# Loads of v moved to GpSimd's queue, output sums in single-bank tiles, and a retuned list schedule, in an attention plus two-MLP kernel

## The chip, the cores and the metric

One core of one Trainium2 chip runs the whole program. The metric is the device time of one execution in microseconds (us), the median of several runs; lower is better.

## What is computed

Attention with a threshold, and then two MLPs, on 4 batches, 8 heads, 576 rows and head size 64 (2304 tokens of width 512, inner width 2048):

```python
scores = scale * np.matmul(q, k.transpose(0, 1, 3, 2))
thresh = np.max(scores, axis=-1, keepdims=True) - tau
scores = np.where(scores >= thresh, scores, -1000000000.0)
scores = scores - np.max(scores, axis=-1, keepdims=True)
attn = np.exp(scores)
attn = attn / (np.sum(attn, axis=-1, keepdims=True) + 1e-09)
x = np.matmul(attn, v)            # heads side by side: (2304, 512)
h = x @ w_in;  g = np.maximum(h, 0.0) + alpha * np.minimum(h, 0.0);  x = g @ w_out
h = x @ w2_in; g = h - np.tanh(h);                                   out = g @ w2_out
```

## The kernel before, in words

The kernel does not run its loops in the order in which they are written. Each piece of work is recorded with `add` (in `Plan`, from line 78): the engines that may do it with a planned duration for each, a rank, what it reads and writes, which PSUM banks it touches, and which tile buffers it takes. `Plan.order` then makes a list schedule: at each step it looks on every engine at the pieces whose inputs are planned to be there, takes the piece that can start first, and among equally early ones the one of lowest rank; where a piece may run on several engines, the engine on which it is planned to start first gets it, after a penalty (`POOL_PEN`, `ACT_PEN`, `DVE_PEN`). The constants at the top of the file (`TA`, `PA`, `PB`, `MLP_PE`, `MLP_G`, `PREP`, `XR`, `OFF`) make the ranks. The instructions of each engine stand in the program in exactly the order found, and each engine works through its own in that order.

The work itself, by stages:

- Attention goes by units: a pair of heads and a block of 256 queries (`prep`, `attend`, `attended`; the 64 left-over queries of a pair in `attend_left`). TensorE makes scores in the PSUM tiles `sc0` and `sc1` (L703, left-over ones L692); VectorE takes row maxima (L576) and a threshold (L579); ScalarE applies it (L305) and the exponential (L586), after which the score tile is free again; VectorE and ScalarE write the weights as two halves of 16 bits (L300, L617, L621), SyncE's queue transposes them by DMA (L631), and TensorE multiplies them by v (L682). The first four units go a shorter way (L597 to L600, L733 to L745).
- v comes by one DMA per head (`load_v`, L550, tile `vs`, three buffers); all but the first four units split it in two more pieces (`rest`, L555, on VectorE or GpSimd). q and k come by L507 and L515, and are split in a high and a low part (L302 or L300 high, L308 low).
- The first MLP's weights come as 32 blocks of 128x512 doubles (`piece`). Each is rebuilt and split by a chain of five steps: L305 and L374 or L372 ("three"), L377 ("middle"), a high part (L300 or L302, tile `i` or `o` and its last block `i3b` and the like) and a low part (L308). The rank of a block is PA plus PB times its number.
- While attention goes on, blocks of 256 tokens that are done pass through the first MLP: input products (`h_pair`, L918, into `hp` or `pt`), and output products (`acc_pair`, L1143, into `acc`). The last two blocks go together (`wide_products`, L1107).
- The second MLP multiplies by a scheme of seven products (`out_products`, L1035, and L1042 for two pairs that go plainly). Its output sums stand in four PSUM banks. Those are the two halves each of `sc0` and `sc1`, which by then serve attention no more: `half_bank` and `two_banks` cut them out. At a block's end ScalarE copies one sum (L300) and VectorE adds up the rest (L1068), and SyncE's queue stores the rows (L1088, L1092 for the last block).
- At the start TensorE gets 220 matmuls that compute nothing of use (`warm`, L1192) wherever the schedule has nothing better.

Of the kernel before, what the change touches and what calls it, by code (L numbers as in the profile page):

```python
# [9 lines left out]
F32 = mybir.dt.float32  # L10
# [21 lines left out]
KW, VW = S, 5 * D  # L32
# [9 lines left out]

TA = 69.2859
PA, PB = -14.922, 21.7041
MLP_PE = 1954.1131
MLP_G = -1037.3118
PREP = 2416.5189
WHOLE, SOLO, NATIVE = 4, 0, 4  # L50
FLEX_R = 1
TX = 240
# [13 lines left out]
FLEX = 1
T_WARM = 0.3
N_WARM = 110
DVE_PEN = 0.5807
OFF = {"KS": -791.84, "S": -573.01, "M": -4327.05, "TH": -2173.26, "E": -1574.86, "X": -552.67, "R": -2860.41, "N": -5093.87, "NL": -258.85, "F": -1836.12, "DT": -6146.31, "T": 21.16, "H": 2659.35, "AV": -799.7, "XC": -548.69, "XH": -2968.53}  # L70
DMA_LAG = 2.2
DMA_RATE = 230e3
BUFS = {
# [165 lines left out]
def attention_mlp_mlp(ctx: ExitStack, tc: tile.TileContext, kv, q0, q1, tau, w1i, w1o, alpha, w2i, w2o, out):  # L239
# [11 lines left out]
    add = plan.add  # L251
# [21 lines left out]

    sc = [ppool.tile([P, 1024], F32, name=f"sc{k}") for k in range(2)]
    acc = [ppool.tile([P, 512], F32, name=f"acc{t}") for t in range(2)]
    hp = ppool.tile([P, 2, BLK], F32, name="hp")
    pt = ppool.tile([P, 4, P], F32, name="pt")

    hps = hp, pt.rearrange("p (k c) s -> p k (c s)", k=2)

# [6 lines left out]
    ROOM = ("room", 0)  # L289
    T = {}  # L290
# [29 lines left out]
    space = []  # L320
# [174 lines left out]
    def prep(u, rank):  # L495
# [48 lines left out]
        for a in range(2) if k == u else ():  # L544
            n = (k, a)
            vs, v3 = ("vs", n), ("v3", n)

            def load_v(e, a=a, vs=vs):
                x = take(tpool, vs, [P, 2, 5, D], F32, "vs", BUFS["vs"])
                e.dma_start(out=x[:, 0], in_=kv[b, h + a][:, S:].rearrange("p (c d) -> p c d", c=5))  # L550

            def rest(e, part, vs=vs, v3=v3):
                x = T[vs][:, part]
                out_ = take(tpool, v3, [P, 5, D], BF16, "v3", BUFS["v3"]) if part else T[vs][:, 1]
                e.tensor_tensor(out=out_, in0=x, in1=x.bitcast(BF16)[:, :, 1::2], op=ALU.subtract)  # L555

            add({"SYNC": rate * VW}, rank - 6, load_v, [ROOM], [(*vs, 0)], takes=[("vs", vs)], lag=DMA_LAG)
            if not one(u):
                for part in range(2):
                    add(either(0.4, 0.7), rank, lambda e, part=part, f=rest: f(e, part), [(*vs, part), ROOM], [v3 if part else (*vs, 1)],  # L560
                        takes=[("v3", v3)] if part else [])
# [449 lines left out]

    def half_bank(n):
        k = {1: 0, 6: 1, 2: 2, 3: 3, 7: 4, 5: 5, 4: 6, 8: 7}[n]
        return sc[k // 4][:, k % 4 * BLK:(k % 4 + 1) * BLK], k // 2

    def two_banks(k):
        return sc[k // 2][:, k % 2 * 512:(k % 2 + 1) * 512]

    def out_products(p, rank):
        m, n = p // NPAIR, p % NPAIR  # L1020
# [58 lines left out]
        for t in (1, 0):  # L1079
            x = 3 - 2 * t  # L1080

            def both(e, t=t, x=x):
                total(e, T[o[t]], two_banks(x), T[o[t]])

            def store(e, t=t):
                if m < 2 * NBLK - 1:
                    row = (m - NBLK) // 2 * S + (m - NBLK) % 2 * BLK + t * P
                    e.dma_start(out=out[row:row + P, :], in_=T[o[t]])  # L1088
                else:
                    for k in range(2):  # L1090
                        row = (2 * t + k + 1) * S - D
                        e.dma_start(out=out[row:row + D, :], in_=T[o[t]][k * D:(k + 1) * D, :])  # L1092

            z = oa + ob if t else oc + od
            add({"DVE": 0.6}, r, both, [("c", x), *z], z, [("c", x)])
            add({"SYNC": 1.2}, r, store, z, [("out", m, t)], lag=3.0)

    def wide_products(p, rank):
        f = p - (NBLK - 2) * NPAIR
        banks = [acc[0], acc[1], two_banks(2), two_banks(3)]  # L1100
        keys = [("acc", 0), ("acc", 1), ("c", 2), ("c", 3)]
        for c in range(4):
            def emit(e, c=c):
                gh, gl = (T["g", p][:, part] for part in range(2))
                hi, lo = (weight(0, "o", part, f // 4)[:, f % 4, c * P:(c + 1) * P] for part in range(2))
                for n, (w, g) in enumerate(((hi, gh), (hi, gl), (lo, gh))):
                    e.matmul(banks[c], lhsT=w, rhs=g, start=(f == 0 and n == 0), stop=(f == NF - 1 and n == 2))  # L1107

            reads = [("w", (0, "o", f // 4), f % 4, part) for part in range(2)]
            add({"PE": 0.69}, rank + MLP_PE, emit, [*reads, ("g", p, 0), ("g", p, 1)], [keys[c]], [keys[c]])  # L1110
        if f < NF - 1:
            return
        for c in (2, 3, 0, 1):
            o = ("o", 2 * (NBLK - 2) + c)
# [208 lines left out]
```

## Time and profile before

| | us |
|---|---|
| median of 3 runs (lowest to highest) | 1052.99 (1048.88 to 1056.25) |
| the profiled execution | 1052.28 |
| its span, first to last instruction | 1050.5 |
| TensorE busy / idle in the span | 1024.3 / 26.2 |
| VectorE busy | 773.1 |
| ScalarE busy | 617.6 |
| GpSimd busy | 75.0 |
| mean granted TensorE clock | 0.993 of full |

In the profile, PE is TensorE's matmuls, PEld its weight loads, DVE is VectorE, ACT is ScalarE, POOL is GpSimd and SP is SyncE; a q behind an engine's name is its queue of DMA issues. A tile's name stands before an arrow, what it is made of behind it. "Idle" is the time an engine stood still before an instruction, and the name behind the arrow is what ended that wait. TensorE is at 2.4 GHz where the granted clock is 1.00 and at 1.2 GHz where it is half.

### The profile page before, as it was taken

Reading aid. Unit: us, or ns where it says so; the run is one execution under the profiler, and the core shown is the slowest. Engines: PE = TensorE matmul, PEld = TensorE weight load, DVE = VectorE, ACT = ScalarE, POOL = GpSimd, SP = SyncE. Lnnn points to the kernel's source line nnn. Section 1 sums busy time; section 2 is a strip of 40 time slices with the busy share of each in tenths; the row PEclk is TensorE's granted clock in tenths of the full one; section 3 lists DMA queues with packets and bytes.
Section 4 is the critical chain, followed back from the end, with each engine's and each line's share of the span. In section 5 each row is a group of like instructions: output and inputs, shape, how many; then the busy total and the mean of one; then the engine's idle time right before and its main releaser. Section 6 shows DMA issues by size and latency. Waiting matters only on the chain.

```text
span 1050.5 us, 22471 instructions
## 1 busy us (share of the span) xinstructions
PE 1024.3 (98%) x8859; PEld 928.7 (88%) x8859; DVE 773.1 (74%) x1738; ACT 617.6 (59%) x1287; POOL 75.0 (7%) x101
## 2 busy tenths in 40 slices
PE   9979889999999999999999999999999999999997
PEld 7759879999989999998999888998898898899886
DVE  6999989878878778887867787674584484485465
ACT  6988988788878788887746554442312222331321
POOL 0122121011110111101100000000000000000000
PEclk9989989999999999999999999999999999999999
DMA  6678988667876657775575343200010010010000
GB/s 201 185 180 192 214 204 172 131 117 153 149 135 135 131 120 146 146 124 119 98 218 185 130 126 115 81 21 1 21 41 21 21 41 21 21 41 21 1 21 21
DMA packets 188889, 110.75 MB, mean 105 GB/s; under 512 B 158688, under 2 KB 171248, under 8 KB 188784
## 3 DMA queue, kind: packets, MB, share of 16 engines
q1 hardware_dynamic: 188480, 108.51, 44.6%
q8 instruction: 69, 1.13, 0.5%
q10 hardware_dynamic: 304, 0.82, 0.3%
q14 instruction: 36, 0.29, 0.1%
HBM read 61.58 MB, written 9.96 MB: 68 GB/s over the span
## 4 chain that ended last, share of the span: by engine, by line
PE 59%; DVE 2%; ACT 2%; issue 1%; DMA 0%; SPq 0%; DVEq 0%; ACTq 0%
PE sc L1035 13%; PE hp L918 10%; PE acc L872 6%; PE pt L918 5%; PE acc L1143 5%; PE sc L1042 5%; PE pt L872 3%; PE hp L872 3%; PE pt L682 2%; PE sc L1107 2%; PE acc L1107 2%; PE sc L703 1%; DVE st L576 1%; ACT e L305 1%; ACT e L586 0%
## 5 line engine op out<-in xcount | busy, mean ns | idle before, releaser
L918 PE MATMUL hp<-x,i 128*128 128x256 f32 (+1 forms) x1584 | 231.5, 291 | 10.8 <-ACT e L305 5.3
L918 PEld LDWEIGHTS hp<-x,i 128*128 128x128 f32 x1584 | 206.5, 191 | 22.4 <-ACT e L305 5.6
L1143 PE MATMUL acc<-g,o 128*128 128x256 f32 x1232 | 165.7, 279 | 0.4 <-POOL g L308 0.4
L1143 PEld LDWEIGHTS acc<-g,o 128*128 128x128 f32 x1232 | 152.7, 188 | 3.9 <-POOL g L308 0.6
L305 ACT ACTIVATE e<-sc,st,qscale 128x576 f32<-128x576 f32 x144 | 118.0, 828 | 33.0 <-DVE st L579 20.8
L1035 PE MATMUL sc<-wp,g 128*128 128x256 f32 x756 | 135.9, 280 | 0.0
L1035 PEld LDWEIGHTS sc<-wp,g 128*128 128x128 f32 x756 | 115.8, 188 | 1.3
L576 DVE TENSOR_REDUCE st<-sc 128x1 f32<-128x576 f32 x144 | 102.7, 750 | 13.4 <-PE sc L703 12.5
L586 ACT ACTIVATE e<-e,natau 128x576 f32<-128x576 f32 x144 | 110.9, 774 | 0.2
L621 DVE SCALAR_TENSOR_TENSOR rw<-e,st,rw 128x576 f16<-128x576 f32 x128 | 103.6, 827 | 9.2 <-ACT rw L300 8.4
L1035 PE MATMUL sc<-wp,rw 128*128 128x256 f32 x378 | 106.1, 281 | 0.8 <-ACT o L300 0.8
L300 ACT ACTIVATE rw<-e,st 128x576 f16<-128x576 f32 x103 | 77.9, 771 | 16.7 <-DVE st L592 7.4
L300 ACT ACTIVATE g<-mr 128x512 fp32r<-128x512 f32 (+1 forms) x99 | 59.1, 597 | 47.8 <-PE sc L1107 16.6
L682 PE MATMUL pt<-eT,vs 128*64 128x256 f16 (+1 forms) x1584 | 72.6, 246 | 0.9 <-DMA eT<-rw 0.9
L1035 PEld LDWEIGHTS sc<-wp,rw 128*128 128x128 f32 x378 | 71.2, 188 | 2.3 <-ACT o L300 1.0
L308 DVE TENSOR_TENSOR g<-mr,g 128x512 fp32r<-128x512 f32 x80 | 55.6, 695 | 19.3 <-ACT g L300 18.4
L682 PEld LDWEIGHTS <-vs 128*64 128x64 bf16 x1584 | 64.5, 111 | 5.3 <-issue 1.0
L703 PE MATMUL sc<-kh,qh 64*128 64x320 f32 (+1 forms) x672 | 62.9, 314 | 4.3 <-ACT e L305 4.1
L872 PE MATMUL acc<-x,i 128*128 128x512 f32 x264 | 65.5, 395 | 0.0
L703 PEld LDWEIGHTS sc<-kh,qh 64*128 64x128 f32 x672 | 50.0, 188 | 13.5 <-ACT e L305 5.1
L872 PEld LDWEIGHTS acc<-x,i 128*128 128x128 f32 x264 | 48.9, 187 | 11.4
L918 PE MATMUL pt<-x,i 128*128 128x256 f32 (+1 forms) x352 | 58.0, 311 | 0.0
(247 smaller groups left out, 1708.4 us busy)
## 6 DMA issues: line engine op xcount, KB each, us to landing
vs<-in_kv_dram SPq DMA_DIRECT2D x58, 160.0 KB, 2.9
rw<-in_w1o_dram SPq DMA_DIRECT2D x16, 512.0 KB, 4.6
rw<-in_w2i_dram SPq DMA_DIRECT2D x16, 512.0 KB, 4.7
rw<-in_w2o_dram SPq DMA_DIRECT2D x16, 512.0 KB, 3.9
rw<-in_kv_dram SPq DMA_DIRECT2D x56, 144.0 KB, 2.9
rw<-in_w1i_dram SPq DMA_DIRECT2D x15, 512.0 KB, 4.9
out_dram<-o SPq DMA_DIRECT2D x16, 256.0 KB, 2.0
x1d<-o SPq DMA_DIRECT2D x14, 256.0 KB, 2.7
```

What stands on the lines that cost most here:

```text
L300: e.activation(out=out_, in_=in_, func=AF.Copy, **({} if scale is None else {"scale": scale}))
L305: e.activation(out=out_, in_=in_, func=AF.Prelu, alpha=alpha, **kw)
L308: e.tensor_tensor(out=out_, in0=in_, in1=hi.bitcast(F32), op=ALU.subtract)
L576: e.tensor_reduce(out=T[st][:, 0, j:j + 1], in_=x(s), axis=AX.X, op=ALU.max, negate=True)
L586: e.activation(out=w_, in_=w_, func=AF.Exp, bias=natau, scale=1.0, accum_out=T[st][:, 2, j:j + 1])
L621: e.scalar_tensor_tensor(out=x_[:, S + D:], in0=w_, scalar=r, in1=x_[:, :S], op0=ALU.mult, op1=ALU.subtract)
L682: e.matmul(po[HALVES[a]], lhsT=plane((k, a), part, c), rhs=eT(a, block), start=(i == 0), stop=(i == len(TERMS) - 1), skip_group_check=True)
L703: e.matmul(to(a, c), lhsT=x[HALVES[a], s], rhs=y[HALVES[a], c], start=(i == 0), stop=(i == len(terms) - 1))
L872: e.matmul(hq[k], lhsT=weight(1, "i", part, f // 4)[:, c, (f % 4) * P:(f % 4 + 1) * P], rhs=slots_of_x[x][:, :, c, :], start=(n0 + i == 0) ...
L918: e.matmul(hq if both_blocks else hq[:, k, :], lhsT=weight(l, "i", part, f // 4)[:, c, (f % 4) * P:(f % 4 + 1) * P], rhs=slots_of_x[x][:, ...
L1035: e.matmul(out_, lhsT=x[:, a], rhs=y[:, b], start=(begins and i == 0 and number in (1, 2, 5, 4)), stop=(n == NPAIR - 1 and i == 2), skip_g ...
L1143: e.matmul(acc[t][:, (c % 2) * BLK:(c % 2 + 1) * BLK], lhsT=w[:, c * P:(c + 1) * P], rhs=g[:, k, :], start=(f == 0 and n == 0 and c % 2 == ...
```

## The change

Four edits in one. The loads of v are recorded for GpSimd, with a planned 1.2 us each, in place of SyncE's queue. The output sums of the second MLP get four tiles of one bank each (`out0` to `out3`), for which the pool that holds `sc0` and `sc1` is released when the first of them is asked for. `SLACK` goes from 0 to 0.067: among pieces that can start up to 67 ns after the earliest, the lowest rank wins. And the ranks and penalties are new numbers.

```diff
-TA = 69.2859
-PA, PB = -14.922, 21.7041
+TA = 67.5699
+PA, PB = -1048.431, 17.9757
...
-POOL_PEN = 0.7718
-ACT_PEN = 0.0
+POOL_PEN = 0.4091
+ACT_PEN = 0.0556
...
-SLACK = 0
+SLACK = 0.067
...
-DVE_PEN = 0.5807
+DVE_PEN = 0.2845
...
-    sc = [ppool.tile([P, 1024], F32, name=f"sc{k}") for k in range(2)]
...
+    spool = tc.alloc_tile_pool(name="spool", bufs=1, space=PSUM)
+    sc = [spool.tile([P, 1024], F32, name=f"sc{k}") for k in range(2)]
+    banks_of_out = []
...
-            add({"SYNC": rate * VW}, rank - 6, load_v, [ROOM], [(*vs, 0)], takes=[("vs", vs)], lag=DMA_LAG)
+            add({"POOL": 1.2}, rank - 6, load_v, [ROOM], [(*vs, 0)], takes=[("vs", vs)], lag=DMA_LAG)
...
-        return sc[k // 4][:, k % 4 * BLK:(k % 4 + 1) * BLK], k // 2
+        return two_banks(k // 2)[:, k % 2 * BLK:(k % 2 + 1) * BLK], k // 2
...
-        return sc[k // 2][:, k % 2 * 512:(k % 2 + 1) * 512]
+        if not banks_of_out:
+            spool.release()
+            mpool = ctx.enter_context(tc.tile_pool(name="mpool", bufs=1, space=PSUM))
+            banks_of_out.extend(mpool.tile([P, 512], F32, name=f"out{n}") for n in range(4))
+        return banks_of_out[k]
```

What the new numbers do shows in the order of the instructions. On VectorE, around the last block of the first MLP's fourth input quarter (its low part is written to `i3b`), before:

```order
L555 TENSOR_TENSOR v_2_1977<-vs_1792 128x320
L308 TENSOR_TENSOR i_1811<-tw_1914,i_1811 128x512
L374 TENSOR_SCALAR rw_1857<-rw_1857 128x512
L589 TENSOR_SCALAR st_1842<-st_1842 128x2
L576 TENSOR_REDUCE st_1993<-sc_90 128x1
L592 RECIPROCAL st_1842<-st_1842 128x2
L377 SCALAR_TENSOR_TENSOR tw_1987<-tw_1987,rw_1857 128x512
L579 TENSOR_SCALAR st_1993<-st_1993,qscale,atau 128x1
L302 TENSOR_SCALAR i_1811<-tw_1987 128x512
L756 SCALAR_TENSOR_TENSOR x_96<-pt,x_95 128x256
L308 TENSOR_TENSOR i3b<-tw_1987,i_1811 128x512
```

and now, on VectorE (lines are two higher here):

```order
L379 SCALAR_TENSOR_TENSOR tw_1839<-tw_1839,rw_1770 128x512
L623 SCALAR_TENSOR_TENSOR rw_1822<-e_1722,st_1559,rw_1822 128x576
L310 TENSOR_TENSOR last<-rw_1090,last 64x64
L557 TENSOR_TENSOR vs_1836<-vs_1836 128x320
L310 TENSOR_TENSOR i3b<-tw_1839,i_1653 128x512
```

with two of its steps now on ScalarE:

```order
L307 ACTIVATE tw_1839<-rw_1770 128x512
L374 ACTIVATE rw_1770<-rw_1770 128x512
L307 ACTIVATE e_1845<-sc_96,st_1830,qscale 128x576
L588 ACTIVATE e_1845,st_1830<-e_1845,natau 128x576
L302 ACTIVATE i_1653<-tw_1839 128x512
```

The step "three" (L374 before, on `rw_1857`) and the high part (L302) of this block went from VectorE to ScalarE, and the block's last instruction, the 270th on VectorE before, is the 240th now.

On GpSimd, in the stretch where the units with three-part v begin, before:

```order
L374 TENSOR_SCALAR rw_797<-rw_797 128x512
L302 TENSOR_SCALAR qh_916<-rw_829 128x256
L308 TENSOR_TENSOR o_879<-tw_884,o_879 128x512
L308 TENSOR_TENSOR last<-rw_716,last 64x64 x2
L555 TENSOR_TENSOR vs_899<-vs_899 128x320
L555 TENSOR_TENSOR v_1_1007<-vs_899 128x320
```

and now:

```order
L552 DMA vs_806<-in_kv_dram 128x320
L304 TENSOR_SCALAR qh_840<-rw_763 128x256
L310 TENSOR_TENSOR qh_840<-rw_763,qh_840 128x256
L557 TENSOR_TENSOR vs_806<-vs_806 128x320
L310 TENSOR_TENSOR o_801<-tw_855,o_801 128x512
L304 TENSOR_SCALAR o_801<-tw_922 128x512
L304 TENSOR_SCALAR kh<-rw_763 128x576
L552 DMA vs_1018<-in_kv_dram 128x320
L310 TENSOR_TENSOR qh_899<-rw_827,qh_899 128x256
L552 DMA vs_1029<-in_kv_dram 128x320
L310 TENSOR_TENSOR g_1040<-mr,g_1040 128x512
L557 TENSOR_TENSOR vs_1018<-vs_1018 128x320
```

The loads of v (L552) stand between splits of q, k, weights and g. Over the whole program GpSimd goes from 93 to 201 instructions beside its preamble: 58 loads and 50 more splits.

On TensorE, the last matmuls of the program, the plain pair of the last block's output, before:

```order
L1042 MATMUL sc0_89<-wp0_10255,g_1_13500 128x512 x2
L1042 MATMUL sc0_89<-wp1_10256,g_1_13500 128x512
L1042 MATMUL sc0_89<-wp0_10255,g_1_13500 128x512 x2
L1042 MATMUL sc0_89<-wp1_10256,g_1_13500 128x512
L1042 MATMUL sc1_90<-wp0_10255,g_1_13500 128x512 x2
L1042 MATMUL sc1_90<-wp1_10256,g_1_13500 128x512
L1042 MATMUL sc1_90<-wp0_10255,g_1_13500 128x512 x2
L1042 MATMUL sc1_90<-wp1_10256,g_1_13500 128x512
```

and now:

```order
L1048 MATMUL out1_105<-wp0_10278,g_1_13511 128x512 x2
L1048 MATMUL out1_105<-wp1_10279,g_1_13511 128x512
L1048 MATMUL out1_105<-wp0_10278,g_1_13511 128x512 x2
L1048 MATMUL out1_105<-wp1_10279,g_1_13511 128x512
L1048 MATMUL out3_107<-wp0_10278,g_1_13511 128x512 x2
L1048 MATMUL out3_107<-wp1_10279,g_1_13511 128x512
L1048 MATMUL out3_107<-wp0_10278,g_1_13511 128x512 x2
L1048 MATMUL out3_107<-wp1_10279,g_1_13511 128x512
```

The twelve matmuls are the same, but they write tiles of their own (`out1`, `out3`), while ScalarE's copy and VectorE's first four sums read `out0` and `out2`.

## Rows read from the trace of the kernel before

**Rows 1.** Part 1 of the page: busy time of three engines, share, instructions.
```profile
PE 1024.3 (98%) x8859; PEld 928.7 (88%) x8859; DVE 773.1 (74%) x1738; ACT 617.6 (59%) x1287; POOL 75.0 (7%) x101
```

**Rows 2.** Six stretches: us; PE, PEld, DVE, ACT, POOL busy; PEclk, DMA share, GB/s.
```profile
0.00:60.00 60.00, 58.95 (x497) 44.02 (x499) 48.46 (x117) 48.07 (x98) 8.11 (x18) 1.00 0.68 205
60.00:140.00 80.00, 67.58 (x718) 61.73 (x714) 74.89 (x163) 70.32 (x148) 17.52 (x21) 0.92 0.84 189
140.00:200.00 60.00, 58.42 (x636) 54.34 (x634) 52.58 (x111) 52.15 (x109) 9.51 (x10) 0.99 0.78 169
200.00:500.00 300.00, 295.65 (x3366) 280.20 (x3363) 245.55 (x537) 245.59 (x536) 36.51 (x50) 1.00 0.71 134
500.00:1000.00 500.00, 499.17 (x3361) 448.51 (x3360) 321.85 (x739) 191.16 (x377) 3.36 (x4) 1.00 0.21 64
1000.00:1050.50 50.50, 44.57 (x295) 39.84 (x293) 29.74 (x74) 10.31 (x22) 0.00 (x0) 0.98 0.08 22
```

**Rows 3.** Who PE waited for, the longest: us in total, times, longest.
```profile
PE hp L918 <- ACT e L305: 5.3, 2, 4.4
PE sc L703 <- ACT e L305: 4.1, 5, 1.2
PE hp L918 <- DVE i L302: 2.1, 1, 2.1
```

**Rows 4.** Timeline of PE around its two stalls: start us, us, what, [idle before].
```profile
74.78 2.68 PE L918 MATMUL hp<-x,i 128*128 128x256 f32 x11 [4.35 <-ACT e L305]
...
123.35 1.06 PE L703 MATMUL sc<-kh,qh 64*128 64x320 f32 x11 [1.16 <-ACT e L305]
...
125.65 2.16 PE L682 MATMUL pt<-eT,vs 128*64 128x256 f16 x36
...
130.78 1.06 PE L692 MATMUL sc<-kh,last 128*128 128x320 f32 x6 [1.28 <-ACT e L305]
...
134.49 0.80 PE L918 MATMUL hp<-x,i 128*128 128x256 f32 x2 [2.07 <-DVE i L302]
```

**Rows 5.** One stretch, DVE alone: us, DVE busy (instructions), PEclk, DMA share, GB/s.
```profile
0.00:134.70 134.70, 118.98 (x270) 0.97 0.76 194
```

**Rows 6.** View of tile vs: count, ns min/median/max, first to last start.
```profile
L550 SPq DMA_DIRECT2D vs<-in_kv_dram x58: 327/424/1249, 4.7 to 530.2; - x58
...
L555 DVE TENSOR_TENSOR vs<-vs x32: 475/490/962, 57.2 to 533.5; 128x320 f32<-128x320 f32 x32
L555 POOL TENSOR_TENSOR vs<-vs x18: 713/722/2175, 70.5 to 517.2; 128x320 f32<-128x320 f32 x18
```

**Rows 7.** The loads of v, L550: us from issue to landing.
```profile
DMA to landing us min/median/max: 2.1/2.9/7.8
```

**Rows 8.** Timeline: a second load of a unit on SP, and that unit's first product.
```profile
264.93 1.73 SPq L550 DMA_DIRECT2D vs<-in_kv_dram  x2
...
275.19 2.16 PE L682 MATMUL pt<-eT,vs 128*64 128x256 f16 x36
```

**Rows 9.** What POOL waited for, the longest entry.
```profile
POOL qh L308 <- ACT qh L300: 85.9, 10, 15.1
```

**Rows 10.** Timeline of the program's end on PE.
```profile
1041.44 0.96 PE L1042 MATMUL sc<-wp,g 128*128 128x512 f32 x3 [0.47 <-ACT o L300]
1042.98 0.97 PE L1042 MATMUL sc<-wp,g 128*128 128x512 f32 x3 [0.57 <-DVE o L1068]
1044.22 1.67 PE L1042 MATMUL sc<-wp,g 128*128 128x512 f32 x6 [0.28 <-DVE o L1068]
```

**Rows 11.** The same end on DVE.
```profile
1042.50 2.47 DVE L1068 TENSOR_TENSOR o<-sc,o 128x256 f32<-128x256 f32 x5 [2.81 <-PE sc L1042]
1045.93 0.69 DVE L1068 TENSOR_TENSOR o<-sc,o 128x512 f32<-128x512 f32 x1 [0.97 <-PE sc L1042]
```

More of the change, by code (lines that the diff above doesn't have):

```diff
@@ L41 @@
 STRASSEN = (0, 2, 3, 4, 5, 6)
-TA = 69.2859
-PA, PB = -14.922, 21.7041
-MLP_PE = 1954.1131
-MLP_G = -1037.3118
-PREP = 2416.5189
+TA = 67.5699
+PA, PB = -1048.431, 17.9757
+MLP_PE = 1433.9332
+MLP_G = -1384.7596
+PREP = 2365.4859
 WHOLE, SOLO, NATIVE = 4, 0, 4
@@ L64 @@
 GRP = 2
-XR = -5767.685
+XR = -5410.2762
 FLEX = 1
@@ L68 @@
 N_WARM = 110
-DVE_PEN = 0.5807
-OFF = {"KS": -791.84, "S": -573.01, "M": -4327.05, "TH": -2173.26, "E": -1574.86, "X": -552.67, "R": -2860.41, "N": -5093.87, "NL": -258.85, "F": -1836.12, "DT": -6146.31, "T": 21.16, "H": 2659.35, "AV": -799.7, "XC": -548.69, "XH": -2968.53}
+DVE_PEN = 0.2845
+OFF = {"KS": -535.86, "S": 778.7, "M": -3424.39, "TH": -4738.67, "E": -2104.47, "X": 647.63, "R": -3288.83, "N": -2846.97, "NL": 1041.57, "F": -2998.86, "DT": -6288.94, "T": 881.05, "H": 1417.61, "AV": 252.54, "XC": -843.71, "XH": -2688.93}
 DMA_LAG = 2.2
@@ L1091, in store @@
                         row = (2 * t + k + 1) * S - D
-                        e.dma_start(out=out[row:row + D, :], in_=T[o[t]][k * D:(k + 1) * D, :])
+                        e.dma_start(out=out[row:row + D, :], in_=T[o[t]][HALVES[k], :])
             z = oa + ob if t else oc + od
@@ L1099, in wide_products, with home_of @@
         f = p - (NBLK - 2) * NPAIR
-        banks = [acc[0], acc[1], two_banks(2), two_banks(3)]
+        def home_of(c):
+            return acc[c] if c < 2 else two_banks(c)
         keys = [("acc", 0), ("acc", 1), ("c", 2), ("c", 3)]
@@ L1106, in emit @@
                 for n, (w, g) in enumerate(((hi, gh), (hi, gl), (lo, gh))):
-                    e.matmul(banks[c], lhsT=w, rhs=g, start=(f == 0 and n == 0), stop=(f == NF - 1 and n == 2))
+                    e.matmul(home_of(c), lhsT=w, rhs=g, start=(f == 0 and n == 0), stop=(f == NF - 1 and n == 2))
             reads = [("w", (0, "o", f // 4), f % 4, part) for part in range(2)]
@@ L1116, in drain @@
             def drain(e, c=c, o=o):
-                copy(e, take(apool, o, [P, 512], F32, "o", BUFS["o"]), banks[c])
+                copy(e, take(apool, o, [P, 512], F32, "o", BUFS["o"]), home_of(c))
             def store(e, c=c, o=o):
```

## The prediction

> **What bounds the kernel now.** I read the share of busy time first, then a table by stretches, then the list of TensorE's waits, and last the timeline at the two places where TensorE stands still. TensorE is busy 98% of the span and no other engine over 74% [rows 1], so only TensorE's lost time can be won, 26.2 us of idle, and what a low clock costs. The table by stretches says where that is [rows 2]. From 500 to 1000 us TensorE lacks 0.83 us: no gain there, whatever the order. From 200 to 500 it lacks 4.35 us. From 60 to 140 it lacks 12.42 us, at a mean granted clock of 0.92, which is full speed with two stretches at half (1.2 instead of 2.4 GHz), each behind a long wait. In that same stretch VectorE is busy 74.9 of 80 us and ScalarE 70.3: they bound it, by what they must finish before TensorE can go on. From 0 to 60 TensorE looks full, but part of that is the 220 warm-up matmuls; VectorE and ScalarE set the pace there too (48 of 60 us each, of which the first 10 are loads). The end lacks 5.93 us.
>
> The waits agree: TensorE waits longest for ScalarE to free a score tile and for a weight block's high part from VectorE [rows 3]. The timeline has them at 74.78 (4.35 us), and from 123 to 134.49 (1.16, 1.28, 2.07 us) [rows 4]. The last of these is the fourth input quarter of the first MLP: its high part is on VectorE behind softmax work.
>
> **The change part by part.** The sum is made against the profiled execution, 1052.28 us (span 1050.5 and 1.78 outside); it lies 0.7 below the median of 1052.99, which I let go.
>
> *The new ranks, 60 to 140 us.* The block's last VectorE instruction ends some 0.7 us after 134.70, and is the 270th on VectorE; by 134.70 VectorE had been busy 118.98 us, so it had been idle 15.7 us since the start [rows 5]. In the new order it is the 240th. Priced kind by kind with the durations of before (an instruction that changed engine at the mean of its kind on the new one), the VectorE work up to it is 107.9 us in place of 119.6: 11.7 us less. But TensorE comes to that matmul with less work behind it too. Four attention steps that stood ahead of it now stand behind it: one scores, one products, one left-over scores and one left-over products, 6.0 us together (the first three begin in rows 4 with 1.06, 2.16 and 1.06 us, a few matmuls each not counted). So the block is ready 11.7 us earlier and wanted 6.0 us earlier: 5.7 us less waiting at most. Against it stands GpSimd: 53 of its instructions now stand ahead of that point where 28 did, and they disturb VectorE. The same split that takes VectorE 490 ns at the median took 962 ns at the worst [rows 6], so each of the 25 costs VectorE between nothing and 0.47 us, 0 to 11.8 us. I let 7 of the 25 collide, 3.3 us, since the median shows no delay at all. That leaves 2.4 us, and with no collision 5.7; I take 3.5, as the half-clock stretch that follows the wait goes with it in part. Both ends are kept: -5.7 to +6.1 (all 25 collide).
>
> *The first 70 us.* At the 11th scores matmul, for which both orders have put the same work on TensorE, VectorE has 2.5 us and ScalarE 4.4 us more ahead than before, counted in the same way, since high parts of weights went to ScalarE. That scores matmul will be 2.5 to 4.4 us later. I cost it at nothing: right behind it the old order waits 4.35 us for ScalarE [rows 4], and in the new one the matmul that waits there has 0.9 us of VectorE work and 3.5 us of ScalarE work more ahead, less than the 4.35, so the delay falls into that wait. If the wait does not shrink, 4.4 us are lost.
>
> *200 to 500 us.* With 8 to 13 us less work ahead on VectorE and ScalarE at equal TensorE progress (counted between 240 and 300 us of TensorE work), the waits there should shrink. TensorE lacks 4.35 us [rows 2]; what remains are waits for freed tiles, so I take 1.2 of it, between 0 and 4.35.
>
> *The loads of v.* 58 issues leave SyncE's queue, 0.42 us each [rows 6]; TensorE waits for none of that queue's transposes for long, so nothing is gained. On GpSimd no row shows a DMA issue. Below, it is no dearer than the shortest on SyncE, 0.33; above, than the longest GpSimd instruction over the same 320 columns, 2.18 [rows 6]; nearest is the median of that instruction, 0.72. Total GpSimd work becomes 75 [rows 1] + 50 splits (32 us) + 58 x 0.72 (42 us) = 149 us within 540 us: no bound. What counts is lateness. A unit's second load must wait for a buffer that the unit before frees, and is wanted soon: issued at 264.93, first used at 275.19, 10.3 us [rows 8]. Over the 25 second loads from the fifth unit on, that time has a median of 9.7 us and 4.3 us at the shortest. The chain in it is 2.9 us to landing [rows 7] and two splits of 0.49 [rows 6], 3.9 us, so 5.8 us are spare. While such a load waits for its buffer, splits of q, k, weights and g stand behind it on GpSimd, and TensorE's scores and input products wait for those. I cost it at nothing, covered by those 5.8 us; gone, that cover costs a us per us and unit.
>
> GpSimd and VectorE do lock each other out: the 713 ns split took 2175 ns once [rows 6], 1.46 us more. If every load were late by that, two of the 25 would be too late or just in time, about 1.1 us in all. The Trainium skill, page "SBUF — State Buffer", section "SBUF: two separate sides", speaks against this edit: a DMA from GpSimd's queue needs descriptors that GpSimd writes itself, and it cannot write them while VectorE holds the shared port; the section below it, "A bandwidth-pool intuition that's wrong", gives 3100 ns for a load that takes 620 alone. By that figure each load would be 2.5 us late, three of the 25 would run out of their spare time, for an estimated 3.5 us, and the sum would be 1049.4. The trace agrees that the two engines lock; no run here yet shows a DMA from that queue.
>
> *Single-bank tiles.* In the middle of the second MLP they win nothing (0.83 us in 500). At the end they do. The last twelve matmuls stand still three times, 0.47, 0.57 and 0.28 us, for ScalarE and VectorE reading the other bank of the same tile, and start up anew each time [rows 10]; they end at 1045.89, 4.9 us after the work before them. In one run, at the pace of the last six (1.67 us for 6), they take some 3.2 us: 1.7 less. VectorE's last sum waits for them (0.97 us) [rows 11]; its five sums before it then run beside the matmuls, done by about 1043.9, so the matmuls still end last. -1.7 us, between -1.3 (the idle alone) and -2.0.
>
> *Sum:* 1052.28 - 3.5 - 0 - 1.2 - 1.7 = 1045.9, or 1046.
>
> **The rivals.**
>
> *All stalls go (faster).* For it: the deficit of the fourth quarter, 5.7 us, is larger than the wait of 2.07 us it shows. Then the 12.42 us of 60 to 140 go but for the first wait of 4.35 (8.1), and so do 1.6 of the next 60 us and 1.3 after [rows 2], and 1.7 at the end: 12.7 less, 1039.6. Against it: the first 70 us are heavier than before.
>
> *Only the end is won (no change).* VectorE is lengthened by the doubled GpSimd work, or ScalarE's 4.4 us at the start are never caught up; then the 3.5 and the 1.2 fall away and 1050.6 stays. For it: VectorE is at 94% from 60 to 140, so each lengthening shows in full. The lock-out of loads by VectorE, 1.1 us by the rows, ends here too.
>
> *Late v (slower).* GpSimd works in order, and has stood 15.1 us in a single wait for ScalarE [rows 9]. A load of v behind such a wait comes late, and TensorE stands before that unit's products. It decides from 5.8 us of delay on, where the spare time is used up. At 6.4 us on the mean over 25 units it costs 25 x 0.6 = 15 us; with the end's gain and no other, 1052.28 + 15 - 1.7 = 1065.6. Against it: the ten waits of that row are 8.6 us on the mean, and in the new order few loads stand behind a split that waits for ScalarE.
>
> **How the numbers follow.** The forecast (1042.5 to 1049) has 0.46, all stalls gone 0.24, only the end 0.18, late v 0.12. One per cent, about what a measurement of this kernel can tell from no change, is 10.5 us: below 1042.5 is faster, above 1063.5 slower. All of the second case and a rest of the first, 0.07, fall below: 0.31 faster. Late v is split, 0.10 above: 0.10 slower, 0.59 within. The range goes from 1037 (the second case with some 2 us more of 200 to 500) to 1059 (the no-change case with the load delays and most of the 6.1 us of collisions); the forecast's own is 1042.5 to 1049.
>
> **What would show it.** Right: in the table by stretches 60 to 140 lacks some 9 us in place of 12.4, one of the two half-clock stretches is shorter or gone, and the wait for the fourth quarter's high part is no longer listed; the last twelve matmuls run without a gap. Wrong: a wait of TensorE's products for `vs` or its splits, or waits of scores for `kh` from GpSimd, among the longest; VectorE's split at over 0.49 us at the median; a DMA issue on GpSimd that takes over 2 us; a first wait at 75 us as long as before and the scores matmul behind 73.

## The result, and the profile after

| | before | after |
|---|---|---|
| median, us (lowest to highest, runs) | 1052.04 (1048.88 to 1056.25, 4) | 1065.18 (1064.12 to 1065.82, 4) |
| ratio, 95% interval | | 1.0120 (1.0104 to 1.0137) |
| the profiled execution / its span | 1052.28 / 1050.5 | 1065.82 / 1064.0 |
| TensorE busy / idle in the span | 1024.3 / 26.2 | 1031.9 / 32.1 |

The changed kernel is 1.2% slower, 13.1 us. The forecast was no change, 1046.0, with a range to 1059; the result lies outside it. Of the 13.5 us between the two spans TensorE is idle for 5.9 and busy 7.6 longer. Up to 5.4 of the 7.6 are the clock, by an estimate: its mean in the profiled execution is 0.988 where it was 0.993, which loses 12.8 us of full speed ((1 - 0.988) x 1064.0) in place of 7.4.

First the shares, and the table of the same six stretches [rows 1, 2], after (us; PE, PEld, DVE, ACT, POOL busy; PEclk, DMA share, GB/s):

```profile
PE 1031.9 (97%) x8859; PEld 934.4 (88%) x8859; DVE 772.6 (73%) x1710; ACT 611.0 (57%) x1265; POOL 148.9 (14%) x209
```

```profile
0.00:60.00 60.00, 56.04 (x453) 42.01 (x453) 44.05 (x103) 45.33 (x86) 14.73 (x30) 1.00 0.65 196
60.00:140.00 80.00, 69.08 (x665) 62.13 (x666) 72.47 (x149) 68.67 (x145) 25.70 (x32) 0.92 0.77 188
140.00:200.00 60.00, 57.18 (x638) 52.46 (x633) 50.66 (x107) 47.16 (x101) 15.67 (x19) 0.94 0.76 150
200.00:500.00 300.00, 294.24 (x3318) 278.66 (x3318) 240.90 (x520) 232.27 (x499) 76.14 (x112) 0.99 0.68 133
500.00:1000.00 500.00, 496.35 (x3417) 445.95 (x3418) 327.68 (x740) 202.20 (x403) 16.62 (x18) 1.00 0.23 68
1000.00:1064.00 64.00, 59.03 (x381) 53.20 (x379) 36.80 (x94) 15.34 (x34) 0.00 (x0) 0.98 0.06 17
```

TensorE lacks 3.96, 10.92, 2.82, 5.76, 3.65 and 4.97 us in them; before it lacked 1.05, 12.42, 1.58, 4.35, 0.83 and 5.93. So the stretch that I looked at, 60 to 140, is 1.5 us better and the end 1 us; every other one is worse. (The stretches are cut by time, and the changed kernel is some 7 us behind in them, so they do not hold quite the same work.) The half clock (1.2 GHz) spread too: 140 to 200 has 0.94 where it had 0.99, and 400 to 450, with the longest wait below, 0.97 where it had 1.00:

```profile
400.00:450.00 50.00, 46.21 (x542) 44.20 (x541) 37.04 (x79) 34.76 (x74) 12.97 (x19) 0.97 0.65 118
```

Note VectorE from 0 to 60: 44.05 us of work where it did 48.46.

Who TensorE waits for now, the longest [rows 3]:

```profile
PE hp L920 <- DVE mr L941: 7.1, 3, 3.8
PE sc L705 <- ACT e L307: 3.0, 5, 1.3
PE out L1041 <- DVE o L1074: 1.9, 3, 0.6
PE hp L920 <- ACT i L302: 1.6, 1, 1.6
PE hp L920 <- ACT x L302: 1.6, 1, 1.6
```

The 4.4 us for ScalarE's `e` is gone, but three long waits for VectorE's hidden rows stand in its place, and three in the second MLP that were not there. No wait for `vs` is in the list.

A table of waits doesn't say when the loss arises, since a delay can be made good later. So I put the two traces side by side by TensorE's own progress: each group of matmuls that the program emits together counts with its shortest duration among the kernels compared, warm-ups left out, and the table gives how much later than in the kernel before TensorE begins the same amount of work (us; the kernels e2 to e17 are those of the next section). It is worked out from the one profiled execution of each kernel, and that is not always near the median: after took 1065.82 us in it, e2 1061.47, e8 1059.33, where the medians are 1065.18, 1058.41 and 1062.98.

```
work done  time before   after   e2     e8     e3     e6    e11    e16    e17
    2         13.5       +7.3   +6.9   +7.5   +0.6   +6.6   +0.4   +0.4   +0.0
   10         27.0       +6.4   +6.0   +6.5   +0.6   +6.5   +0.4   +0.3   +0.0
   15         35.8       +6.8   +6.4   +7.0   +0.6   +6.6   +6.4   +0.3   +0.0
   40         77.5       +6.8   +6.4   +7.2   +0.5   +6.1   +6.2   -0.2   -0.5
   60         98.5       +6.3   +5.5   +6.1   +0.8   +5.7   +5.7   +0.0   -1.1
   65        103.7       +6.4   +5.5   +6.2   +0.8   +6.0   +6.6   +7.7   +0.0
  120        172.0       +6.9   +6.6   +6.8   +0.6   +6.0   +7.5   +5.8   -0.5
  300        360.6       +9.4   +8.5  +10.2   +2.3   +5.8   +8.8   +8.8   +0.2
  380        444.9      +12.9   +8.0   +9.9   +2.2   +5.8   +7.7  +10.4   +0.2
  600        670.4      +12.6   +8.0   +8.8   +0.4   +5.4   +8.1   +8.0   -0.1
  960       1030.6      +15.3  +10.7   +8.8   +0.4   +5.4   +8.1   +8.0   -0.1
```

After: 7 us are lost by the time TensorE has done 2 us of work, 6 more come by the middle of the attention, and 2.7 in the second MLP; the end gives 2 back. The first are at the very beginning, on SyncE and VectorE:

```profile
0.74 0.88 SPq L358 DMA_DIRECT2D rw<-in_w1i_dram  x2
1.67 1.74 SPq L509 DMA_DIRECT2D rw<-in_q_dram  x2
3.45 0.68 SPq L1174 DMA_DIRECT2D tau_sb<-in_tau_dram  x1
```

```profile
11.71 0.43 DVE L376 TENSOR_SCALAR rw<-rw 128x512 int32<-128x512 uint32 x1 [11.71 <-DMA rw<-in_w1i_dram]
```

Two weight loads of 512 KB each now stand ahead of q and tau, and VectorE's first instruction is a weight's step that waits for such a load until 11.71 us. Before, it began at 3.4 us with tau. q itself lands late as well. The first scores on TensorE and the first row maxima on VectorE, before and after:

```profile
6.62 2.06 PE L703 MATMUL sc<-rw 64*128 64x320 f32 x8
8.30 1.42 DVE L576 TENSOR_REDUCE st<-sc 128x1 f32<-128x576 f32 x2 [4.32 <-PE sc L703]
```

```profile
12.02 1.21 PE L705 MATMUL sc<-rw 64*128 64x320 f32 x6 [1.07 <-DMA rw<-in_q_dram]
15.36 1.42 DVE L578 TENSOR_REDUCE st<-sc 128x1 f32<-128x576 f32 x2
```

The scores end 4.55 us later (13.23 for 8.68), and the row maxima, behind the weight's steps, begin 7.1 us later. TensorE is hardly idle meanwhile, since its warm-up matmuls fill the gap; so little of this loss shows as idle time.

Of the next 6 us, 2.5 come between 172 and 361 us, most of them (1.9) in e2 as well, which has the same order with v on SyncE's queue. The other 3.5 come with one stall at 433 us. On SP, POOL, DVE and PE:

```profile
424.36 3.51 SPq L633 DMA_TRANSPOSE eT<-rw  x2
```

```profile
424.49 1.14 POOL L552 DMA_DIRECT2D vs<-in_kv_dram  x2 [3.30 <-PE pt L684]
```

```profile
431.90 0.52 DVE L619 TENSOR_SCALAR rw<-e,st 128x576 f16<-128x576 f32 x1 [3.75 <-DMA eT<-rw]
432.34 0.87 DVE L941 SCALAR_TENSOR_TENSOR mr<-mr,nalpha,hp 128x256 f32<-128x256 f32 x2
```

```profile
433.35 2.17 PE L920 MATMUL hp<-x,i 128*128 128x256 f32 x11 [3.79 <-DVE mr L941]
```

Two transposes on SyncE and two loads of v on GpSimd begin side by side; VectorE stands 3.75 us at the head of its queue until a transpose has let go of a buffer, the hidden rows stand behind it, and TensorE waits 3.79 us. No engine is slow here, a transfer is. The stall comes back wherever the changed order loads v from GpSimd's queue, with another length in each execution: 3.79 us here, 2.83 in e5, 1.78 in e9 and 1.34 in e8. In e2 and e18, whose order is the same there and whose v is on SyncE's queue, TensorE has no such wait.

The third is in the second MLP, three times in this form:

```profile
774.25 2.40 POOL L310 TENSOR_TENSOR x<-rw,x 128x1024 fp32r<-128x1024 f32 x1 [225.37 <-ACT x L302]
```

```profile
774.79 2.02 DVE L985 TENSOR_TENSOR gs<-gs,mr 128x128 f32<-128x128 f32 x1
```

```profile
779.54 0.39 PE L1041 MATMUL out<-wp,rw 128*128 128x256 f32 x1 [0.62 <-DVE o L1074]
```

The low part of x moved to GpSimd, and beside it a VectorE instruction of 0.29 us takes 2.02.

Such collisions are not confined to the second MLP. Counting VectorE's instructions that take over 0.15 us longer than the median of the same line and form, there are 32 of them, 21.4 us too long in all, where before there were 23 and 9.2 us; every one of them, before and after, runs beside an instruction of GpSimd. One pair, where VectorE's step has a median of 0.16 us:

```profile
123.47 1.95 POOL L310 TENSOR_TENSOR kh<-rw,kh 128x576 fp32r<-128x576 f32 x1 [0.65 <-issue]
```

```profile
124.04 1.41 DVE L591 TENSOR_SCALAR st<-st 128x2 f32<-128x2 f32 x1
```

And the end [rows 10, 11] on PE and DVE:

```profile
1056.11 2.92 PE L1048 MATMUL out<-wp,g 128*128 128x512 f32 x12
```

```profile
1056.02 2.53 DVE L1074 TENSOR_TENSOR o<-out,o 128x256 f32<-128x256 f32 x5 [1.03 <-ACT o L302]
1059.07 0.69 DVE L1074 TENSOR_TENSOR o<-out,o 128x512 f32<-128x512 f32 x1 [0.52 <-PE out L1048]
```

The last twelve matmuls run without a gap, 2.92 us, as forecast.

### The profile page after: what moved, and what is told of

The parts are those of the page before. It is cut to its first block, busy times and chain, and to the rows that moved or that the text cites. A ratio compares the mean times of both kernels' runs of the same rounds, so it can differ in the third digit from the quotient of the medians.

```text
span 1064.0 us, 22530 instructions
## 1 busy us (share of the span) xinstructions
PE 1031.9 (97%) x8859; PEld 934.4 (88%) x8859; DVE 772.6 (73%) x1710; ACT 611.0 (57%) x1265; POOL 148.9 (14%) x209
## 5 line engine op out<-in xcount | busy, mean ns | idle before, releaser
L1041 PE MATMUL out<-wp,g 128*128 128x256 f32 x756 | 135.9, 280 | 0.0
L1041 PEld LDWEIGHTS out<-wp,g 128*128 128x128 f32 x756 | 115.8, 188 | 1.3
L1041 PE MATMUL out<-wp,rw 128*128 128x256 f32 x378 | 106.3, 281 | 1.9 <-DVE o L1074 1.9
L302 ACT ACTIVATE g<-mr 128x512 fp32r<-128x512 f32 (+1 forms) x91 | 54.1, 595 | 56.5 <-PE out L1115 16.6
L302 ACT ACTIVATE rw<-e,st 128x576 f16<-128x576 f32 x86 | 65.6, 770 | 23.0 <-DVE st L594 10.8
L684 PE MATMUL pt<-eT,vs 128*64 128x256 f16 (+1 forms) x1584 | 75.5, 251 | 1.6 <-DMA eT<-rw 1.1
L1041 PEld LDWEIGHTS out<-wp,rw 128*128 128x128 f32 x378 | 71.2, 188 | 3.8 <-DVE o L1074 2.5
L310 DVE TENSOR_TENSOR g<-mr,g 128x512 fp32r<-128x512 f32 x76 | 53.1, 699 | 14.0 <-ACT g L302 12.9
L310 POOL TENSOR_TENSOR x<-rw,x 128x1024 fp32r<-128x1024 f32 x3 | 7.2, 2406 | 394.2 <-ACT x L302 394.2
L941 DVE SCALAR_TENSOR_TENSOR mr<-mr,nalpha,hp 128x256 f32<-128x256 f32 x112 | 49.0, 474 | 16.3 <-ACT mr L934 15.7
```

The source lines that it names most:

```text
L302: e.activation(out=out_, in_=in_, func=AF.Copy, **({} if scale is None else {"scale": scale}))
L310: e.tensor_tensor(out=out_, in0=in_, in1=hi.bitcast(F32), op=ALU.subtract)
L684: e.matmul(po[HALVES[a]], lhsT=plane((k, a), part, c), rhs=eT(a, block), start=(i == 0), stop=(i == len(TERMS) - 1), skip_group_check=True)
L1041: e.matmul(out_, lhsT=x[:, a], rhs=y[:, b], start=(begins and i == 0 and number in (1, 2, 5, 4)), stop=(n == NPAIR - 1 and i == 2), skip_g ...
```

## The experiments

The order is a list that the program works out while it is built, so three kinds of edit are possible: leave the list as it is and change one thing at its emission (e1, e2, e3, e7, e10), rearrange the list by hand (e5, e6, e9, and the grafts of e11, e16, e17), or change what the planner works from and get a new list (e4, e8, e12 to e15, e18). The first kind measures a cause by itself.

**Which part of the change, e1 to e4.** e1 and e2 move only the queue of the loads of v, in either order:

```diff
 # e1, on the kernel before
-                e.dma_start(out=x[:, 0], in_=kv[b, h + a][:, S:]...)
+                nc.gpsimd.dma_start(out=x[:, 0], in_=kv[b, h + a][:, S:]...)
 # e2, on the changed kernel
-                e.dma_start(out=x[:, 0], in_=kv[b, h + a][:, S:]...)
+                nc.sync.dma_start(out=x[:, 0], in_=kv[b, h + a][:, S:]...)
 # e3, on the kernel before: sc in a pool of its own, out0 to out3 in four single banks (as in the change)
 # e4, on the kernel before: all the new numbers, TA to OFF, and SLACK = 0.067
```

e1: 

> The kernel before, its order of instructions unchanged on every engine, only the 58 loads of v issued from GpSimd's queue. Theory A (the new numbers make a worse order; the queue is innocent): 1050 to 1054, the same as before. Theory B (the queue: loads of v late behind GpSimd's waits, its splits late behind the loads): 1058 to 1066.

e2: 

> The changed kernel, its order unchanged, only the 58 loads of v issued from SyncE's queue again. Theory A: 1062 to 1067, no better than the changed kernel. Theory B: 1050 to 1056. If the GpSimd queue takes half of the loss: about 1058.

e3: 

> The kernel before with the single-bank tiles alone; the order of instructions is unchanged. Both theories: the last twelve matmuls in one run of about 2.9 us in place of 4.9, 1050.0 to 1051.5, 2 us less. If the single-bank tiles cost something in the second MLP: 1052 or more.

e4: 

> The kernel before with all the new numbers (ranks, penalties, SLACK 0.067), loads of v on SyncE, two-bank tiles. Theory A: 1062 to 1069 (the loss of the changed kernel, without the 2 us of its end). Theory B: 1049 to 1054.

| | median, us | ratio to before, 95% interval |
|---|---|---|
| e1 before, v on GpSimd's queue | 1057.39 | 1.0058 (1.0038 to 1.0079) |
| e2 after, v on SyncE's queue | 1058.41 | 1.0063 (1.0040 to 1.0085) |
| e3 before, single-bank tiles | 1049.06 | 0.9970 (0.9959 to 0.9981) |
| e4 before, new numbers | 1073.22 | 1.0202 (1.0176 to 1.0228) |

Neither theory had it alone. The queue costs 5.6 us in the old order (1057.39 - 1051.82; 4 to 8 by the interval) and 6.8 in the new (1065.18 - 1058.41). The single-bank tiles win 2.8. The new order by itself, e2 against e3, loses 9.4. Together 6.8 + 9.4 - 2.8 = 13.4, the loss seen; as the three are steps from one kernel to the next, they had to add up, and the sum confirms nothing by itself. e3 is faster than both kernels, and the best version of this study. e4 missed upwards: with the loads on SyncE and the new numbers the planner makes another order again, and that one is worse than the changed kernel's.

**Why the queue costs 6 us, e1, e7, e10.** Three ways were open: GpSimd stands in its queue until a buffer is free, with splits behind it (my rival "late v"); loads and transposes from two queues run beside each other; or only GpSimd's own transfers do harm. e7 issues the loads from a third queue. In e10 GpSimd waits in the load's place, but loads nothing:

```diff
 # e7, on the kernel before
-                e.dma_start(out=x[:, 0], ...)
+                nc.scalar.dma_start(out=x[:, 0], ...)
 # e10, on the kernel before, ahead of the load on SyncE
+                nc.gpsimd.memset(x[:, 0, 4, D - 1:], 0.0)
```

e7: 

> The kernel before, its order unchanged, the 58 loads of v issued from ScalarE's queue. Theory overlap (a load of v from any second queue runs beside SyncE's transposes on the same 16 DMA engines and slows both): transposes that run beside a load of v land in 2.7 to 3.0 us after their issue at the median in place of 2.1, and the time is 1057 or more (ScalarE also pays 58 issues). Theory GpSimd (only its queue, or its splits behind a waiting load, is slow): transposes at 2.0 to 2.2 us; the time is then ScalarE's price alone.

e10: 

> The kernel before, loads of v on SyncE as there; only a one-element memset on GpSimd stands ahead of each load, so that GpSimd waits for the buffer in the load's place, with its splits queued behind, as it does when it issues the load. Theory blocked (the loss by the queue is GpSimd's in-order wait): 1056 to 1059. Theory transfers (the loss is in how GpSimd's loads and SyncE's transposes land beside each other): 1051 to 1053, transposes at 2.1 us.

e7 took 1052.03 us, 0.9998 (0.9980 to 1.0017), and e10 1053.09, 1.0008 (0.9996 to 1.0019). So the blocked GpSimd costs at most 2 us. That it did wait, for 67.0 us in all where e1's waited for 81.7, stands in e10's list of GpSimd's waits, here with e1's under it (us in total, times, longest):

```profile
POOL vs L550 <- PE pt L683: 67.0, 13, 14.2
```

```profile
POOL vs L550 <- PE pt L682: 81.7, 15, 14.5
```

What e10 leaves out is the transfers, and with them GpSimd's own time for an issue (0.55 us at the median in e1, where e10's memset takes 0.10). From 60 to 560 us the view of DMA has, for the kernel before, e1 and e7 in this order (line, queue, times, KB each, median us from issue to landing; and the queue that carries v: packets, MB, share):

```profile
vs<-in_kv_dram SPq DMA_DIRECT2D x49, 160.0 KB, 2.9
...
eT<-rw SPq DMA_TRANSPOSE x128, 3.5
```

```profile
q0 software_dynamic: 2352, 8.03, 7.1%
...
vs<-in_kv_dram POOLq DMA_DIRECT2D x49, 160.0 KB, 3.8
...
eT<-rw SPq DMA_TRANSPOSE x128, 3.8
```

```profile
q10 hardware_dynamic: 7056, 8.03, 6.3%
...
vs<-in_kv_dram ACTq DMA_DIRECT2D x49, 160.0 KB, 3.1
...
eT<-rw SPq DMA_TRANSPOSE x128, 3.6
```

From GpSimd a load lands 0.9 us later and a transpose 0.3; from ScalarE 0.2 and 0.1. Split by whether a load of v is under way beside it, a transpose lands, after its issue has ended, in 2.08 us at the median before and 2.95 in e1 (2.34 in e7); with no load beside it in 2.03, 2.02 and 2.03. In the new order it is the same: 2.75 beside a load in the changed kernel, 2.04 in e2. So the transposes are late where the two overlap. One load of v is 144 packets on ScalarE's queue (7056 / 49) and 48 on GpSimd's (2352 / 49): a third as many, three times as large. By the Trainium skill, page "DMA: Bandwidth & Descriptors", section "Queues, rings and completion order", each DMA engine takes its queues in turn and empties a whole packet before it turns to the next. The trace agrees so far as a transpose beside GpSimd's larger packets is 0.87 us later and beside ScalarE's smaller ones 0.26. That the size of the packets is the cause was not tried by itself, and GpSimd's time for the issues stays a rival of it. How TensorE loses the time in the old order is not shown either: e1's profiled execution is longer by only 2.2 of the 5.6 us, no wait for `vs` is in it, and TensorE's waits for transposes are 2.2 us there for 0.9 before, but 1.7 in e7 too, which loses nothing. In the new order the place is known. The stall at 433 us is by transposes: the two took 7.2 us to land there at the median (5.9 in e5, 4.8 in e9, 4.5 in e8), and the same two in e2 and e18, which have no stall, 3.3 and 3.5.

**The first instructions, e5, e6, e9.** Both kernels' first hundred instructions sorted the other way round, and a graft: the old list's first 200 entries, then the new list's others in their order, with buffers dealt out anew (this moved no other entry).

```diff
 # e5, on the changed kernel
         order = plan.order()
+        n = 1 + max(k for k, (i, e) in enumerate(order) if i in (318, 320))
+        order[:n] = sorted(order[:n], key=lambda x: 118 <= x[0] < 309)
 # e6, on the kernel before
         order = plan.order()
+        n = 1 + max(k for k, (i, e) in enumerate(order) if 117 < i < 131)
+        order[:n] = sorted(order[:n], key=lambda x: 0 if x[0] in (1, 2, 117, 309) else 1 if 117 < x[0] < 131 else 2)
 # e9, on the changed kernel; FIRST holds the old list's first 200 entries
         order = plan.order()
+        first = [(int(x[1:]), {"E": "PE", "A": "ACT", "D": "DVE", "G": "POOL", "S": "SYNC"}[x[0]]) for x in FIRST.split()]
+        order = plan.mend(first + [x for x in order if x[0] not in {i for i, _ in first}])
```

e5: 

> The changed kernel, only the first hundred instructions sorted anew: what belongs to the first weight block (two of its loads on SyncE, its steps on ScalarE and VectorE) stands behind the first unit's softmax, as in the kernel before; all later instructions in the changed order. Theory start (the 6 to 7 us that the attention is late after 20 us are never caught up): 1058 to 1061. Rival (VectorE at 60 to 140 us is the bound, the late start is hidden there): 1064 to 1066.

e6: 

> The kernel before, only its first hundred instructions sorted anew: two weight loads ahead of q and tau on SyncE, the first weight pieces ahead of the first softmax on ScalarE and VectorE. Theory start: 1057 to 1060. Rival: 1051 to 1053.

e9: 

> The changed kernel; its first 200 operations (of 4617, about the first 25 us) stand in the order and on the engines of the kernel before, the rest follows in the changed order. Theory start (what the attention is late after 20 us is late at the end): 1057 to 1061, with TensorE's progress at 25 us within 1 us of the kernel before. Rival (the order behind it is what loses): 1063 to 1066.

e6 took 1058.24 us, 1.0054 (1.0036 to 1.0072). In the old order, weights ahead of the first softmax cost 6.0 us, and the progress table has them from the first row to the last: +6.6 at 13.5 us, +5.4 at 1030. VectorE begins like this in it and is busy 6.38 of the first 20 us where it was 10.28 before:

```profile
5.30 0.43 DVE L374 TENSOR_SCALAR rw<-rw 128x512 int32<-128x512 uint32 x1 [5.30 <-DMA rw<-in_w1i_dram]
11.40 0.69 DVE L377 SCALAR_TENSOR_TENSOR tw<-tw,rw 128x512 int32<-128x512 int32 x1 [5.67 <-ACT rw L372]
```

So in the old order a late start is never caught up. (The imitation is not exact: with 36 warm-ups ahead of its first scores, where the changed kernel has 70, TensorE stands still for 2.85 us in e6, and its clock is 0.83 over the first 20 us, 1.00 in the other two kernels.) But the way back does not work: e5 took 1067.41 (2.2 more, the second unit's softmax now stands behind the weights that I bunched), and e9 1063.94, 1.2 less. Its start is the old one, and yet it loses. Where, the next group shows.

**How far the loss reaches, e11, e16, e17, e18, and x on VectorE, e8.** All are the changed kernel. e8 puts the low parts of x on VectorE, e18 that and the loads of v on SyncE, and e11, e16 and e17 graft the old list's first 200, 600 and 1130 entries (about 27, 100 and 200 us) onto e18.

```diff
 # e8; in e18, e11, e16 and e17 together with e2's edit
-        add({"DVE": 1.14, "POOL": 2.4}, rank, lo, ...)
+        add({"DVE": 1.14}, rank, lo, ...)
 # e11, e16, e17: FIRST as in e9, with 200, 600, 1130 entries
```

e8: 

> The changed kernel, with the three low parts of x in the second MLP (128x1024, 2.40 us each on GpSimd) on VectorE as in the kernel before. Theory (GpSimd's long split holds up VectorE's next instruction by 1.7 us, and TensorE's output products wait 0.62 us three times): 1.9 us less, 1063.0 to 1063.6, and the three waits are gone. Rival (VectorE then needs 1.1 us more itself): 1065 to 1066.

e11: 

> The changed kernel with three things undone: loads of v on SyncE, the three low parts of x in the second MLP on VectorE, the first 200 operations in the order of the kernel before; the rest of the new order and the single-bank tiles stay. If the three carry the loss: 1065.2 - 6.8 - 2.2 - 6.0 = 1050.2 (1048 to 1053). If the rest of the new order loses by itself: 1056 or more.

e16: 

> As e11 (loads of v on SyncE, x of the second MLP on VectorE), but with the first 600 operations, about the first 100 us, in the order of the kernel before. If what remains is lost in the first 100 us (weights ahead of the attention, VectorE idle): 1049 to 1053. If it is lost behind them: 1056 or more.

e17: 

> The same with the first 1130 operations, about 200 us. If what remains is lost before 200 us: 1049 to 1052, the kernel before with the single-bank tiles' gain. If the new order loses from 200 to 500 us as well: 1053 to 1056.

e18: 

> The changed kernel with the loads of v on SyncE and the low parts of x of the second MLP on VectorE; the rest of the new order and the single-bank tiles stay. If the two losses add: 1065.2 - 6.8 - 2.2 = 1056.2 (1055 to 1057.5), and what lies between this and the 1052.6 of e17 is lost before 200 us. If they overlap: 1057.5 to 1059.

| | median, us | ratio to before, 95% interval |
|---|---|---|
| e8 after, x on VectorE | 1062.98 | 1.0088 (1.0064 to 1.0112) |
| e18 after, x and v back | 1057.90 | 1.0062 (1.0049 to 1.0076) |
| e11 the same, first 200 entries old | 1059.03 | 1.0062 (1.0047 to 1.0077) |
| e16 the same, first 600 old | 1058.21 | 1.0057 (1.0036 to 1.0077) |
| e17 the same, first 1130 old | 1052.59 | 1.0003 (0.9989 to 1.0016) |

In e8 and e18 the three waits of 0.62 us are gone, and in the progress table e8 stays level through the second MLP (+8.8 at its beginning and at its end) where after goes from +12.6 to +15.3. The times can't resolve it: 2.2 less in e8, 0.5 less in e18 than in e2.

e17 is the kernel that settles the place: with the old order up to 200 us, 5.3 us are gone (1057.90 - 1052.59), so they are lost ahead of 200 us. e11 and e16 say how: the progress table has them level with before up to the border, and then +6.4 at 36 us in e11, +7.7 at 104 us in e16. Wherever the new order takes over, it has weights standing ahead of the attention that the old one has not yet brought in, and must first wait for them. In e16, on PE and DVE:

```profile
106.74 2.69 PE L961 MATMUL hp<-x,i 128*128 128x256 f32 x11 [5.96 <-DVE mr L982]
```

```profile
103.23 1.20 DVE L420 SCALAR_TENSOR_TENSOR tw<-tw,rw 128x512 int32<-128x512 int32 x1 [3.55 <-ACT rw L415]
```

VectorE stands at a weight's step that waits for ScalarE's, and that for the load; the hidden rows stand behind it. So the grafts do not divide the loss further between 0 and 200 us, since each pays at its border. e17 itself lies between the two ranges expected of it. What is left between e17 and e3, 3.5 us of medians, is put to the order from 200 to 500 us by these times alone; e17's profiled execution (span 1048.4) does not show it, and it stays open.

**Single numbers, e12 to e15.** The planner makes a new list for each.

```diff
 # e12, on the kernel before
-PA, PB = -14.922, 21.7041
+PA, PB = -1048.431, 17.9757
 # e13, on the changed kernel: the reverse
 # e14, on the kernel before: SLACK = 0.067
 # e15, on the changed kernel: SLACK = 0
```

e12: 

> The kernel before with the ranks of the first MLP's weights alone (PA, PB) as in the changed kernel; the planner makes its order anew. Theory start (VectorE waits at the beginning for weights that are loaded ahead of q, and never gets the time back): VectorE's first instruction at 10 us or later, 1057 to 1061. Rival (the ranks of the weights are harmless, the other numbers lose): 1050 to 1054.

e13: 

> The changed kernel with PA and PB of the kernel before; the planner makes its order anew. Theory start: tau and q are loaded first again, VectorE begins at 3.4 us, and 5 to 7 us of the loss are gone: 1057 to 1061. Rival: 1064 or more.

e14: 

> The kernel before with SLACK 0.067 alone; the order is made anew. If the wait for a higher rank is harmless: 1049 to 1055. If it carries a part of the loss: 1057 or more.

e15: 

> The changed kernel with SLACK 0; the order is made anew, with the same weights first. Theory start: 1062 to 1069, no better. If SLACK carries the loss: 1050 to 1058.

e12 took 1060.57 us (1.0080, 1.0051 to 1.0108), e13 1072.01 (1.0184, 1.0144 to 1.0224), e14 1064.12 (1.0117, 1.0094 to 1.0139) and e15 1083.89 (1.0298, 1.0270 to 1.0326). PA alone brings the weights ahead of q and loses 8 us, as the theory had it. But e13, with the old start, is 7 us worse than the changed kernel, e14 loses 11 by SLACK alone, and e15 shows that the new numbers need the SLACK that e14 shows to be bad for the old ones. In e13, e14 and e15 TensorE is busy 77.47, 81.25 and 79.67 of the 100 us from 100 to 200, before 93.01. The numbers are one set: a single one of them has no price of its own, and nothing of the 9 us can be put down to one. My expectations took them for separable: e15 lies outside both of its ranges, and e13 and e14 lie far up in the open ends of their second ones.

## Why the prediction was wrong, step by step

- *The first 70 us, "I cost it at nothing"*: this step failed, and with it the next. I counted how much work VectorE and ScalarE have ahead of a matmul, 2.5 and 4.4 us more, and let it fall into the first wait. I did not look at when the first input lands. The new order loads weights ahead of q and tau, the first row maxima begin 7.1 us later, and TensorE is 7 us late after 2 us of work and 6.8 late at 77 us, behind the place where the wait was to swallow it. e6 shows that such a start costs 6.0 us to the end in the old order, and e17, with the old order up to 200 us, gets 5.3 back in the new one.
- *The new ranks, 60 to 140 us, -3.5*: the work was sized well and the idle time was not. Up to the low part of the fourth quarter's last block VectorE does 111.4 us of work in 240 instructions (107.9 forecast, with 3.3 for collisions), but that instruction begins at 132.89: 21.5 us idle where I kept the 15.7 of before. The collisions that I allowed for did come, and were more: 11 instructions and 7.0 us up to there, 6 and 2.1 before, so 4.9 us more for the 3.3. TensorE's waits for that quarter are 1.15, 1.63 and 0.64 us, more than the 2.07 that was to go. The stretch lacks 10.92 us, not the 9 forecast.
- *200 to 500 us, -1.2*: it lacks 5.76 in place of 4.35, 1.4 more; the stall at 433 us, made by transfers, is 3.79 of it. But in e2, which has no such stall, it still lacks 4.29, so the gain did not come there either.
- *The loads of v, 0*: this step failed too, and is about half of the loss: they cost 5.6 to 6.8 us. The issue on GpSimd takes 0.57 us at the median and 0.70 at the longest (0.72 forecast), GpSimd's total is 148.9 (149 forecast, and met by luck: the issues took 33 us for 42, the added splits 41 for 32), and TensorE never waits for `vs`: the spare time holds, and "late v" with its wait for a buffer fell with e10, though its 1065.6 is near the time measured, by chance. What I missed is that a transfer can slow others: I priced the loads' own lateness and none for the transposes that run beside them.
- *The Trainium skill's rule on GpSimd's DMAs and the shared port*, page "SBUF — State Buffer", section "A bandwidth-pool intuition that's wrong", 1049.4 by it: no issue took over 0.70 us, and the loads land at 3.9 us at the median where they took 2.9, 1.0 us later for an estimated 2.5 by the rule. That VectorE held them up is not shown. By that page's section "SBUF: two separate sides" the port that the two engines share is held by one of them for a whole instruction; with that the trace agrees: 0.29 us became 2.02 beside GpSimd's 2.40.
- *GpSimd's work, "no bound"*: true as a sum, but its instructions hold VectorE up, the three low parts of x among them, 1.9 us of TensorE's waits that I had not priced in the second MLP, which I took as full "whatever the order".
- *Single-bank tiles, -1.7*: right. The twelve matmuls take 2.92 us for 4.9, 2.0 less, and e3 measures 2.8 (0.19 to 0.41%).

VectorE's split of v has a median of 0.489 us as before, but as a sign of collisions it was badly chosen, since they fall on other instructions. The range was too narrow because the case at its upper end added neither a loss at the start, not even the 4.4 us named, nor any price for transfers beside each other.

## What to carry to other kernels

Where an engine bounds a stretch, its idle time ahead of that stretch counts as much as its work: read from the order what it waits for first, and which loads stand ahead of that one. A load moved to another queue is not moved out of the way; look at what it will run beside, and at how late that lands, transposes above all. And numbers that steer a list schedule hold only as a set: take another part (here the tiles, which win 0.3%) without them.

## What was not expected of the hardware

- A load of 160 KB goes in 48 packets from GpSimd's queue and in 144 from ScalarE's. Transposes beside the former land 0.87 us later at the median, beside the latter 0.26, and only GpSimd's cost time (e1 +5.6 us, e7 -0.2).
- Two loads and two transposes issued side by side from 424.4 us on took 6.7 and 7.2 us to land (medians of the two), where from one queue they take 2.9 and 3.5. It varies: the same four took 3.6 and 4.5 us in e8.
- A VectorE instruction of 128x128 elements took 2.02 us in place of 0.29 while GpSimd worked on 128x1024. No VectorE instruction took over 0.15 us longer than the median of its kind, before or after, but beside an instruction of GpSimd.
